# State products in runs of three units, reads in the spare output bank: a schedule change in a fused cross-attention and ReGLU kernel

## The chip, the cores and the metric

The kernel runs on one core of a Trainium2 chip. The metric is device microseconds of one execution, taken as the median of several runs; smaller is better. The profile comes from one further execution, recorded by the hardware profiler.

## What is computed

For each of 8 batches and 8 heads there are 512 tokens `x` (64 wide) and 32 state vectors `state`. Tokens read from the states and states read from the tokens; the two results are joined along the rows, heads are folded into the width (8 x 64 = 512), and a feed-forward block with a rectified gate follows.

```python
# x: (8, 8, 512, 64)   state: (8, 8, 32, 64)
scores = scale * x @ state.T                # tokens to states
a = softmax(scores);   xread = a @ state
scores2 = scale * state @ x.T               # states to tokens
a2 = softmax(scores2); sread = a2 @ x
h = concat([xread, sread], axis=2)          # 544 rows per batch and head
rows = h.transpose(0, 2, 1, 3).reshape(8 * 544, 512)
out = (relu(rows @ w_gate) * (rows @ w_val)) @ w_out     # d_ff = 1536
```

The output is 4352 x 512 in float32. Matmul operands on the chip are bf16.

## The kernel before, in words

The 512 token rows of a batch are not multiplied with the gate and value weights directly. Since `xread = a @ state`, the kernel forms the **state products** U = state times weight once per batch (32 states of 8 heads against 1536 columns, for both weights), and then `a` times U. U is stored in bf16 as (weight w, half kc of the heads, column).

The engines work so. TensorE (PE) does all matmuls and transposes. ScalarE (ACT) does the exponentials, relu and copies out of PSUM. VectorE (DVE) does sums, the gate-times-value product and copies. GpSimd (POOL) converts the inputs and issues some loads; SyncE (SP) issues the others, the transposing DMAs and the stores.

The work is a list of **steps**. A step is one block of 128 columns of d_ff, `jf` 0 to 11, of one batch `b`; its number is g = 12*b + jf. In each step PE runs:

- `gv` (L317, matmuls at L314): four matmuls 128x128x512, two for the gate and two for the value, into two PSUM banks. `relu` (L338, ACT) reads the first bank, `mult` (L342, DVE) the second and the relu's result.
- an **output piece**, `out_piece(b, i)` (matmuls at L351): four of the twelve matmuls that make one output tile of 128 rows. A tile is three pieces, i, i+1, i+2 with i a multiple of 3. Its first piece calls `o_bank` for a PSUM bank, and its last is followed by `fin_x`: a copy on ACT (L359) and a store on SP (L360). The piece issued in step g is number g - 18 (`lag`), again counted in twelves per batch.
- then the **units** that are hung on this step by `at(b, jf, f, ...)`, in the order in which they were added.

The units, with their lines:

- `att_half(b, i)`: scores of one half of the heads (L198, PE), exponential (L205, ACT), sum, reciprocal and scaling (L211, L213, L217, DVE); after the second half the result is transposed by a DMA on SP (L225) into ANS, the stationary partner of U in `gv`.
- `u_block(b, lo)`: state products of 512 columns. It calls `u_unit` (eight matmuls of a 64x32 tile of the array, L289, into two banks) for each weight, and `u_out` (L299) to cast each bank into U: both banks of the gate on ACT, both of the value on DVE. So a run is two units, and a batch has three runs.
- `sr(b)`: the states' read of batch b: 32 matmuls of a 128x32 tile (L262, PE), then `sr_norm` on DVE: a reciprocal (L269) and a multiplication into `sn` (L271).
- `sr_T(b)`: one transpose of `sn` (L275, PE) and a copy on ACT (L276).
- `x_dma`, `x_next`, `x_pad`: load of the tokens of a later batch (SP), conversion on POOL and a transposing DMA on SP, and a padded copy on POOL for the read.
- `state_prep`: transposes of the states of batches 4 to 7 on PE (L127) and copies on ACT (L131).

**Banks.** PSUM has eight banks. `bank(name, kind)` (L81) hands them out: kind "r" goes round banks 0 to 5, kind "o" alternates banks 6 and 7 for output tiles. A bank handed out again is waited for until its last reader is through. The counter of each kind is in `turn`.

Steps up to 27 are an order written out by hand, with the banks of each word. The loop of the change begins at step 28, (2,4), and ends with step 107; steps 96 to 107 are those of the states' rows (`gvs`). Orders within an engine's queue are those of the program.

Of the kernel before, what the change touches and what calls it, by code (L numbers as in the profile page):

```python
# [16 lines left out]
def kernel(  # L17
# [9 lines left out]
    nc = tc.nc  # L27
# [7 lines left out]
    NF = d_ff // 128  # L35
# [19 lines left out]
    NK = 2  # L55
# [7 lines left out]
    NX, DP = 2, 66  # L63
# [15 lines left out]
    given, turn = [], {"r": 0, "o": 0}  # L79

    def bank(name, kind="r"):  # L81

        if given:
            n = given.pop(0)
        else:
            n = turn["r"] % 6 if kind == "r" else 6 + turn["o"] % 2
            turn[kind] += 1
        return psum.tile([128, 512], FP32, name=name, tag=f"b{n}")

    held = {}  # L90
# [33 lines left out]
    def state_T(g):  # L124
        ps = held["st", g] = bank("stT_ps").bitcast(BF16)[:, 0:512]
        for i in range(4):
            nc.tensor.transpose(ps.rearrange("p (q i m) -> p q i m", i=4, m=8)[:, :, i],  # L127
                                st_b[:, g % 3, i].rearrange("p h d -> p (h d)"), id128)
# [31 lines left out]
    def x_T(b, j):  # L160

        if b not in xT:
            xT_alloc(b)
        ps = bank("xT_ps").bitcast(BF16)[:, 0:512].rearrange("p (c t) -> p c t", c=NC)
        for c in range(NC):
            if b == 0 and j < 2:
                nc.tensor.transpose(ps[:, c], x_head(b)[:, c, 2 * j:2 * j + 2].rearrange("p h d -> p (h d)"), id128)
            else:
                v, h = (x_tail(b), 2 * j - HK) if b == 0 else (xb[b], 2 * j)
                for h2 in range(2):  # L170
                    nc.tensor.transpose(ps[64 * h2:64 * h2 + 64, c], v[:, c, h + h2], id128)  # L171
        held["xT", b, j] = ps
# [4 lines left out]
    def x_T2(b, half):  # L177
        if b not in xT:
            xT_alloc(b)
        ps = held["xT2", b, half] = bank("xT_ps").bitcast(BF16).rearrange("p (c j t) -> p c j t", c=NC, j=2)  # L180
        for j in range(2):
            for c in range(NC):
                for h2 in range(2):
                    nc.tensor.transpose(ps[64 * h2:64 * h2 + 64, c, j], xb[b][:, c, 4 * half + 2 * j + h2], id128)  # L184
# [68 lines left out]
            src = src.rearrange("p c h d -> p h c d")  # L253
            nc.gpsimd.tensor_copy(out=v[:, hs:hs + src.shape[1]], in_=src)  # L254

    def sr_mm(b):

        ps = held["sr", b] = bank("sr_ps")[:, 0:2 * DP].rearrange("p (r d) -> p r d", r=2)
        for c in range(NC):
            for parity in range(2):  # L260
                for j in range(NJ):
                    nc.tensor.matmul(ps[32 * j:32 * j + 32, parity, 0:D + 1], e_sn[b][:, parity, c, 32 * j:32 * j + 32],  # L262
                                     xa[:, b % NX, H * c + 2 * j + parity, 0:D + 1],
                                     start=(c == 0 and parity == 0), stop=(c == NC - 1), skip_group_check=True)

    def sr_norm(b):
        ps = held["sr", b]
        rr = small.tile([128, 2], FP32, name="rr", tag="rr")
        nc.vector.reciprocal(out=rr, in_=ps[:, :, D])  # L269
        sn = held["sn", b] = small.tile([128, 2, D], BF16, name="sn", tag="sn")  # L270
        nc.vector.tensor_tensor(out=sn, in0=ps[:, :, 0:D], in1=rr.to_broadcast([128, 2, D]), op=ALU.mult)  # L271
# [20 lines left out]
    def u_unit(b, w, lo):  # L292

        u_alloc(b)
        ps = held["u", b, w, lo] = [bank("up"), bank("up")]
        u_mm(ps, b, w, lo, 512)

    def u_out(b, w, lo, kc, eng):
        copy[eng](out=U[b][:, w, kc, lo:lo + 512], in_=held["u", b, w, lo][kc])  # L299
# [17 lines left out]
    def gv(b, jf):  # L317
        if b not in hsb:
            hsb[b] = hpool.tile([128, NF, S], BF16, name="h_sb", tag="h_sb")
        held["gv", b, jf] = [bank("gv_ps"), bank("gv_ps")], hsb[b][:, jf], S  # L320
        for w in range(2):
            for kc in range(NK):
                gv_mm(held["gv", b, jf][0], b, jf, w, kc)

    def gvs(jf):
        f0 = jf * 128
        ps = [bank("gv_ps"), bank("gv_ps")]
        nt = B * Ns
        for w, wsb in ((0, wg_sb), (1, wv_sb)):
            for j in range(NJ):  # L330
                nc.tensor.matmul(ps[w][:, 0:nt], wsb[:, j, f0:f0 + 128], br[:, j].rearrange("p b n -> p (b n)"),  # L331
                                 start=(j == 0), stop=(j == NJ - 1))
        held["gv", B, jf] = ps, hs_sb[:, jf], nt

    def relu(b, jf):
        ps, dst, n = held["gv", b, jf]
        g_sb = held["g", b, jf] = gpool.tile([128, 512], BF16, name="g_sb", tag="g_sb")
        nc.scalar.activation(out=g_sb[:, 0:n], in_=ps[0][:, 0:n], func=AF.Relu)  # L338

    def mult(b, jf):  # L340
        ps, dst, n = held["gv", b, jf]
        nc.vector.tensor_tensor(out=dst, in0=ps[1][:, 0:n], in1=held["g", b, jf][:, 0:n], op=ALU.mult)  # L342
# [4 lines left out]
    def out_mms(src, b, tsub, jfs):  # L347
        if jfs[0] == 0:
            held["o", b, tsub] = o_bank()
        for jf in jfs:  # L350
            nc.tensor.matmul(held["o", b, tsub], src[:, jf, tsub * 128:(tsub + 1) * 128], wo_sb[:, jf],  # L351
                             start=(jf == 0), stop=(jf == NF - 1))
# [4 lines left out]
    def fin_x(b, tsub, eng="act"):  # L357
        o_sb = opool.tile([128, d_model], FP32, name="o_sb", tag="o_sb")
        copy[eng](out=o_sb, in_=held["o", b, tsub])  # L359
        nc.sync.dma_start(out=out_rows(b, tsub), in_=o_sb)  # L360

    def fin_s(t2):
        outr = out.rearrange("(b s) m -> b s m", s=SP)
        o_sb = opool.tile([128, d_model], FP32, name="o_sb", tag="o_sb")
        nc.scalar.copy(out=o_sb, in_=held["o", B, t2])
        for bq in range(4):
            eng = nc.sync if bq % 2 == 0 else nc.scalar
            eng.dma_start(out=outr[t2 * 4 + bq, S:SP], in_=o_sb[bq * Ns:(bq + 1) * Ns])
# [14 lines left out]
    def out_part(b, i):  # L383
        tsub, q = divmod(i, 3)
        out_mms(hsb[b], b, tsub, list(range(4 * q, 4 * q + 4)))

    def out_piece(b, i):
        out_part(b, i)
        if i % 3 == 2:
            fin_x(b, i // 3)  # L390
# [37 lines left out]
    def spin(n, cols=512):  # L428
        for i in range(n):
# [6 lines left out]
             "sc": att_sc, "ex": att_exp, "nr": att_sum, "nx": att_scale, "aT2": att_T2, "ao2": att_out2, "aT": att_T, "ao": att_out,  # L436
             "c": c_unit, "co": c_out, "u": u_unit, "uo": u_out, "gv": gv, "re": relu, "mu": mult, "o": out_part,
             "of": fin_x, "xn": x_next, "xp": x_pad, "sr": sr_mm, "sn": sr_norm}
    program = """
    dx.1.0.2 dx.1.1.2 stc.0.0.act stc.0.1.dve spin.7 stT.0@0 xc.0.0.dve dw.0.0.128 sto.0.act dw.1.0.128 on xc.0.1.dve  # L440
# [31 lines left out]
        assert not given  # L472


    units = {}

    def at(b, jf, f, *args):
        units.setdefault(NF * b + jf, []).append(lambda: f(*args))

    def u_block(b, lo, engs=("act", "act", "dve", "dve")):  # L480
        for w in range(2):
            u_unit(b, w, lo)
            for kc in range(NK):
                u_out(b, w, lo, kc, engs[2 * w + kc])

    def att_half(b, kc):
        att_up(b, kc)
# [7 lines left out]
        att_scale(b, kc)  # L495

    def sr(b):
        sr_mm(b)
        sr_norm(b)

    def state_prep(lo, hi):
# [2 lines left out]
            state_out(g, "act")  # L504

    first, lag = 2 * NF + 4, 18
    at(2, 4, x_dma, 4, (nc.sync,))
    at(2, 10, state_prep, 4, B)
    for b in range(3, B):
        s, late = b - 1, 2 if b == 3 else 0  # L510
        for i, jf in enumerate((3, 5)):
            at(s, jf + late, att_half, b, i)
        for i, jf in enumerate((7, 9, 11)):
            at(s, jf, u_block, b, 512 * i)
        if b + 1 < B:
            at(s, 9, x_next, b + 1)
            at(s, 9, x_pad, b + 1)
        if b + 2 < B:
            at(s, 10, x_dma, b + 2, (nc.sync,))
    for b in range(B):  # L520
        s, jf = {0: (2, 2), 1: (2, 3), 2: (2, 8), 3: (2, 11)}.get(b, (b - 1, 9))
        if b > 1:
            at(s, jf, sr, b)
        at(*divmod(NF * s + jf + 2, NF), sr_T, b, "act")
    for g in range(first, NF * (B + 1)):
        b, jf = divmod(g, NF)
        gv(b, jf) if b < B else gvs(jf)
        relu(b, jf)
        mult(b, jf)
        if g >= lag:  # L530
            out_piece(*divmod(g - lag, NF))
        for f in units.get(g, ()):
            f()
    for t2 in range(2):
        out_mms(hs_sb, B, t2, list(range(NF)))
        fin_s(t2)
# [33 lines left out]
```

The softmax here doesn't subtract the row's maximum and nothing guards it: scores larger than these inputs give would overflow.

## Time and profile before

| | |
|---|---|
| median of 7 runs | 226.88 us (226.65 to 227.56) |
| the profiled execution | 226.73 us, of which its span 224.9 us |
| PE busy | 219.6 us of the span |
| ACT, DVE, POOL busy | 124.7, 128.3, 53.3 us |
| gv matmuls L314, 384 | 96.6 us busy, 380 ns each |
| piece matmuls L351, 372 | 94.5 us busy, 379 ns each |
| state products L289 in the loop, 64x512, 288 | 14.2 us busy |
| casts of U, L299, DVE and ACT | 36 of 684 ns and 36 of 592 ns |
| longest PE wait | 1.2 us, at the start |

In a timeline line the columns are start and duration in us, engine, line and operation, output and inputs by the program's names, count, and in brackets the idle time ahead of it and what ended it. Matmuls are pipelined, and the profile models their ends, so one matmul's duration of 380 ns overlaps the next; the distance between starts is what a matmul costs. Loads of weights (PEld) run beside matmuls. A busy time is a total over the whole span; an idle time matters only on the engine that sets the end.

### The profile page before, as it was taken

The page shows a single profiled execution, that of the slowest core. Times are in us where ns is not written, and L with a number is a line of the kernel's source. Part 1 is how long each engine was busy: PE and PEld are TensorE (multiplying, and loading weights), DVE is VectorE, ACT ScalarE, POOL GpSimd, SP SyncE. Part 2 cuts the span into 40 slices and gives each one's busy share as a digit, 9 for nine tenths or more (in the row PEclk, how much of TensorE's full clock was granted, in tenths as well). Part 3 has the DMA queues.
Part 4 walks back from the last instruction along what each step waited for, and adds up shares of the span by engine and source line. Part 5 has one row for each costly group of instructions (what it writes and reads, how often), then busy time and mean ns, then how long its engine had stood idle before and what let it go on. Part 6 is the DMA issues. An engine that isn't in the chain of part 4 may idle for free.

```text
span 224.9 us, 4871 instructions
## 1 busy us (share of the span) xinstructions
PE 219.6 (98%) x1967; PEld 105.0 (47%) x1967; DVE 128.3 (57%) x226; ACT 124.7 (55%) x236; POOL 53.3 (24%) x58
## 2 busy tenths in 40 slices
PE   7899999999999999999999999999999999999994
PEld 3444454444544444444444443444444445666543
DVE  3587888667387657754866467656865443222100
ACT  4599877773566655664466455655556444322221
POOL 8798747503343240006000600000000000000000
PEclk9999999999999999999999999999999999999999
DMA  6999999070719612681159213611311111111132
GB/s 149 176 195 196 209 231 278 26 187 3 231 52 199 225 47 69 144 255 51 48 115 252 88 59 66 125 50 47 93 50 47 48 47 50 48 56 75 60 93 93
DMA packets 37799, 25.48 MB, mean 113 GB/s; under 512 B 18864, under 2 KB 33200, under 8 KB 37776
## 3 DMA queue, kind: packets, MB, share of 16 engines
q1 hardware_dynamic: 24912, 16.85, 26.5%
q0 software_dynamic: 11968, 7.47, 21.5%
q10 hardware_dynamic: 896, 0.85, 1.4%
q8 instruction: 15, 0.25, 0.5%
q14 instruction: 8, 0.07, 0.1%
HBM read 18.35 MB, written 8.91 MB: 121 GB/s over the span
## 4 chain that ended last, share of the span: by engine, by line
PE 94%; DMA 3%; ACT 1%; issue 0%; POOL 0%; DVE 0%; POOLq 0%; DVEq 0%
PE o_ps L351 38%; PE gv_ps L314 38%; PE gv_ps L331 5%; PE up L289 4%; DMA xb<-in_x_dram 3%; PE upc L289 2%; PE sc_ps L198 1%; PE sr_ps L262 1%; PE o_ps L377 1%; PE xT_ps L184 1%; PE warm_ps L430 1%; PE aT_ps L233 1%; ACT xT L187 0%; PE srT_ps L275 0%; PE stT_ps L127 0%; PE xT_ps L171 0%
## 5 line engine op out<-in xcount | busy, mean ns | idle before, releaser
L314 PE MATMUL gv_ps<-ans,U 128*128 128x512 bf16 x384 | 96.6, 380 | 0.0
L351 PE MATMUL o_ps<-wo_sb,h_sb 128*128 128x512 bf16 x372 | 94.5, 379 | 0.0
L342 DVE TENSOR_TENSOR h_sb<-gv_ps,g_sb 128x512 bf16<-128x512 f32 x96 | 65.3, 688 | 42.0 <-ACT g_sb L338 40.8
L338 ACT ACTIVATE g_sb<-gv_ps 128x512 bf16<-128x512 f32 (+1 forms) x108 | 63.1, 584 | 47.0 <-PE gv_ps L314 32.3
L351 PEld LDWEIGHTS <-h_sb 128*128 128x128 bf16 x372 | 36.1, 98 | 40.9 <-issue 0.7
L314 PEld LDWEIGHTS <-U 128*128 128x128 bf16 x384 | 34.9, 98 | 41.2 <-issue 4.2
L359 ACT COPY o_sb<-o_ps 128x512 f32<-128x512 f32 x29 | 17.0, 586 | 20.7 <-PE o_ps L351 20.7
L299 DVE CAST U<-up 128x512 bf16<-128x512 f32 x36 | 23.2, 684 | 5.3 <-PE up L289 5.2
L299 ACT CAST U<-up 128x512 bf16<-128x512 f32 x36 | 19.4, 592 | 10.1 <-PE up L289 10.1
L140 POOL CAST xb<-xf 128x1024 bf16<-128x1024 f32 x10 | 10.6, 1084 | 53.4 <-DMA xf<-in_x_dram 52.1
L254 POOL COPY xa<-xb 128x2048 bf16<-128x2048 bf16 (+1 forms) x9 | 15.3, 1710 | 13.4 <-PE sr_ps L262 6.6
L211 DVE TENSOR_REDUCE cs<-e_sn 128x16 f32<-128x512 bf16 x16 | 10.9, 684 | 8.6 <-ACT e_sn L205 8.6
L342 DVE TENSOR_TENSOR hs_sb<-gv_ps,g_sb 128x256 bf16<-128x256 f32 x12 | 5.1, 424 | 15.3 <-PE gv_ps L331 10.5
L205 ACT ACTIVATE e_sn<-sc_ps 128x512 bf16<-128x512 f32 x16 | 9.6, 599 | 5.6 <-PE sc_ps L198 5.5
L309 ACT CAST U<-upc 128x512 bf16<-128x512 f32 (+1 forms) x20 | 9.5, 533 | 1.4 <-PE upc L289 1.3
L289 PEld LDWEIGHTS <-stT 64*32 64x32 bf16 x512 | 4.9, 89 | 11.2 <-issue 10.8
L430 PE MATMUL warm_ps<-hs_sb 128*128 128x512 bf16 x23 | 7.8, 456 | 1.2 <-DVE hs_sb L394 1.2
L217 DVE TENSOR_TENSOR a_sn<-e_sn,rc 128x512 bf16<-128x512 bf16 x12 | 8.3, 692 | 0.6
L198 PEld LDWEIGHTS <-xT 128*128 128x128 bf16 x128 | 5.7, 98 | 3.8 <-ACT xT L175 0.7
L331 PE MATMUL gv_ps<-br,wv_sb 128*128 128x256 bf16 x48 | 7.2, 273 | 0.0
L331 PE MATMUL gv_ps<-br,wg_sb 128*128 128x256 bf16 x48 | 7.2, 273 | 0.0
L289 PE MATMUL up<-wg_sb,stT 64*32 64x512 bf16 x144 | 7.2, 386 | 0.0
(64 smaller groups left out, 129.2 us busy)
## 6 DMA issues: line engine op xcount, KB each, us to landing
out_dram<-o_sb SPq DMA_DIRECT2D x31, 256.0 KB, 2.3
xf<-in_x_dram SPq DMA_DIRECT2D x4, 1024.0 KB, 6.2
wo_sb<-in_moe_w_out_dram POOLq DMA_DIRECT2D x2, 768.0 KB, 15.2
wg_sb<-in_moe_w_gate_dram POOLq DMA_DIRECT2D x5, 256.0 KB, 8.6
wv_sb<-in_moe_w_val_dram POOLq DMA_DIRECT2D x5, 256.0 KB, 10.4
xf<-in_x_dram POOLq DMA_DIRECT2D x1, 1024.0 KB, 15.9
xb<-in_x_dram POOLq DMA_DIRECT2D x3, 256.0 KB, 6.8
xb<-in_x_dram POOLq DMA_DIRECT2D x1, 512.0 KB, 12.3
```

The lines of the kernel that those rows point to most:

```text
L140: copy[eng](out=xb[b][:, :, hs].rearrange("p c h d -> p h c d"), in_=xf[b][:, hs])
L211: nc.vector.reduce_sum(out=cs, in_=e_v, axis=AX.X)
L254: nc.gpsimd.tensor_copy(out=v[:, hs:hs + src.shape[1]], in_=src)
L289: nc.tensor.matmul(dst[parity][32 * j:32 * j + 32], stT[r:r + 64, b, j, 32 * parity:32 * parity + 32], wsb[r:r + 64, j, lo:lo + n], start= ...
L299: copy[eng](out=U[b][:, w, kc, lo:lo + 512], in_=held["u", b, w, lo][kc])
L314: nc.tensor.matmul(ps[w], U[b][:, w, kc, f0:f0 + 128], ANS[b][:, kc].rearrange("p c t -> p (c t)"), start=(kc == 0), stop=(kc == NK - 1))
L331: nc.tensor.matmul(ps[w][:, 0:nt], wsb[:, j, f0:f0 + 128], br[:, j].rearrange("p b n -> p (b n)"), start=(j == 0), stop=(j == NJ - 1))
L338: nc.scalar.activation(out=g_sb[:, 0:n], in_=ps[0][:, 0:n], func=AF.Relu)
L342: nc.vector.tensor_tensor(out=dst, in0=ps[1][:, 0:n], in1=held["g", b, jf][:, 0:n], op=ALU.mult)
L351: nc.tensor.matmul(held["o", b, tsub], src[:, jf, tsub * 128:(tsub + 1) * 128], wo_sb[:, jf], start=(jf == 0), stop=(jf == NF - 1))
L359: copy[eng](out=o_sb, in_=held["o", b, tsub])
L430: nc.tensor.matmul(warm_ps[:, 0:cols], warm[:, 0:128], warm[:, 0:cols], start=True, stop=True)
```

## The change

The state products of batches 3 to 7 are made in two runs of three units in place of three runs of two. `u_block(b, part)` takes three of the six (weight, column) pairs; of each unit the first bank is cast on ACT and the second on DVE. Runs stand at steps (b-1, 7) and (b-1, 10), for batch 3 at (2, 8) and (2, 11). After the units of such a step the next output piece is issued too, and the following step has none; so the run lies between two pieces.

The states' reads of batches 2 to 7 write the bank that the next output tile will get (`kind == "spare"` does not advance the turn), not one of the six. They stand behind the run in the same step: batches 4 to 7 move from step 9 to 10, batches 2 and 3 stay at (2, 8) and (2, 11). `sr_T` follows one step later for batches 4 to 7 (still step 11), two steps later for 2 and 3 as before. Those of batches 0 and 1 stay at (2, 4) and (2, 5).

Batch 3's softmax halves move from steps (2, 5) and (2, 7) to (2, 4) and (2, 6). The load of batch 4's tokens moves from (2, 4) to (2, 6).

```diff
@@ bank @@
         if given:
             n = given.pop(0)
+        elif kind == "spare":
+            n = 6 + turn["o"] % 2
         else:
             n = turn["r"] % 6 if kind == "r" else 6 + turn["o"] % 2
             turn[kind] += 1
@@ sr_mm @@
-    def sr_mm(b):
+    def sr_mm(b, kind="r"):
-        ps = held["sr", b] = bank("sr_ps")[:, 0:2 * DP].rearrange("p (r d) -> p r d", r=2)
+        ps = held["sr", b] = bank("sr_ps", kind)[:, 0:2 * DP].rearrange("p (r d) -> p r d", r=2)
@@ the loop and its units @@
-    units = {}
+    units, paired = {}, set()
-    def u_block(b, lo, engs=("act", "act", "dve", "dve")):
-        for w in range(2):
+    def u_block(b, part):
+        for w, lo in ((0, 0), (1, 0), (0, 512), (1, 512), (0, 1024), (1, 1024))[3 * part:3 * part + 3]:
             u_unit(b, w, lo)
-            for kc in range(NK):
-                u_out(b, w, lo, kc, engs[2 * w + kc])
+            u_out(b, w, lo, 0, "act")
+            u_out(b, w, lo, 1, "dve")
     def sr(b):
-        sr_mm(b)
+        sr_mm(b, "spare")
         sr_norm(b)
-    at(2, 4, x_dma, 4, (nc.sync,))
+    at(2, 6, x_dma, 4, (nc.sync,))
     for b in range(3, B):
-        s, late = b - 1, 2 if b == 3 else 0
+        s, late = b - 1, 1 if b == 3 else 0
         for i, jf in enumerate((3, 5)):
             at(s, jf + late, att_half, b, i)
-        for i, jf in enumerate((7, 9, 11)):
-            at(s, jf, u_block, b, 512 * i)
+        for part, jf in enumerate((8, 11) if b == 3 else (7, 10)):
+            at(s, jf, u_block, b, part)
+            paired.add(NF * s + jf)
     for b in range(B):
-        s, jf = {0: (2, 2), 1: (2, 3), 2: (2, 8), 3: (2, 11)}.get(b, (b - 1, 9))
+        s, jf = {0: (2, 3), 1: (2, 4), 2: (2, 8), 3: (2, 11)}.get(b, (b - 1, 10))
         if b > 1:
             at(s, jf, sr, b)
-        at(*divmod(NF * s + jf + 2, NF), sr_T, b, "act")
+        at(s, jf + (2 if b in (2, 3) else 1), sr_T, b, "act")
+    piece = first - lag
     for g in range(first, NF * (B + 1)):
-        if g >= lag:
-            out_piece(*divmod(g - lag, NF))
+        if piece <= g - lag:
+            out_piece(*divmod(piece, NF))
+            piece += 1
         for f in units.get(g, ()):
             f()
+        if g in paired:
+            out_piece(*divmod(piece, NF))
+            piece += 1
```

## The prediction

> **What bounds the kernel now.** I read the page first: engine totals, then the chain that ended last.
>
> ```profile
> span 224.9 us, 4871 instructions
> PE 219.6 (98%) x1967; PEld 105.0 (47%) x1967; DVE 128.3 (57%) x226; ACT 124.7 (55%) x236; POOL 53.3 (24%) x58
> PE 94%; DMA 3%; ACT 1%; issue 0%; POOL 0%; DVE 0%; POOLq 0%; DVEq 0%
> ```
>
> The end is set by TensorE (PE): 98% busy, 94% of the chain. The view of PE's waits has only 1.2 us and 0.7 us, both ahead of the main loop. So in the loop any PE time saved shortens the run, and any new PE wait lengthens it. Next the PE timeline of two state-product steps (start, duration):
>
> ```profile
> 111.66 1.03 PE L351 MATMUL o_ps<-wo_sb,h_sb 128*128 128x512 bf16 x4
> 112.62 0.41 PE L289 MATMUL up<-wg_sb,stT 64*32 64x512 bf16 x8
> 112.84 0.40 PE L289 MATMUL up<-wv_sb,stT 64*32 64x512 bf16 x8
> 113.17 1.04 PE L314 MATMUL gv_ps<-ans,U 128*128 128x512 bf16 x4
> 114.05 1.03 PE L351 MATMUL o_ps<-wo_sb,h_sb 128*128 128x512 bf16 x4
> 114.91 1.03 PE L314 MATMUL gv_ps<-ans,U 128*128 128x512 bf16 x4
> 115.77 1.03 PE L351 MATMUL o_ps<-wo_sb,h_sb 128*128 128x512 bf16 x4
> 116.73 0.41 PE L289 MATMUL up<-wg_sb,stT 64*32 64x512 bf16 x8
> 116.96 0.40 PE L289 MATMUL up<-wv_sb,stT 64*32 64x512 bf16 x8
> 117.28 0.43 PE L262 MATMUL sr_ps<-xa,e_sn 128*32 128x65 bf16 x32
> 117.65 1.04 PE L314 MATMUL gv_ps<-ans,U 128*128 128x512 bf16 x4
> 118.52 1.03 PE L351 MATMUL o_ps<-wo_sb,h_sb 128*128 128x512 bf16 x4
> ...
> 120.25 1.03 PE L351 MATMUL o_ps<-wo_sb,h_sb 128*128 128x512 bf16 x4
> 121.76 0.23 PE L275 MATMUL srT_ps<-id,sn 128*128 128x128 bf16 x1
> 121.83 1.20 PE L314 MATMUL gv_ps<-ans,U 128*128 128x512 bf16 x4
> 122.87 1.02 PE L351 MATMUL o_ps<-wo_sb,h_sb 128*128 128x512 bf16 x4
> ```
>
> Read starts: a gv group or a piece takes 0.864, a plain step 1.73. Piece to piece with a two-unit run is 2.39: 0.66 over a plain step. The units start 0.225 apart, so two are 0.45 and **entering and leaving the run costs 0.21**. With the read (sr) behind, 118.52-115.77 = 2.75: 1.02. With the transpose srT behind, 122.87-120.25 = 2.62: 0.89.
>
> DVE's timeline of the run with the read, and of step (2,11):
>
> ```profile
> 116.23 0.69 DVE L342 TENSOR_TENSOR h_sb<-gv_ps,g_sb 128x512 bf16<-128x512 f32 x1 [0.84 <-ACT g_sb L338]
> 117.42 1.29 DVE L299 CAST U<-up 128x512 bf16<-128x512 f32 x2 [0.50 <-PE up L289]
> 118.63 0.16 DVE L269 RECIPROCAL rr<-sr_ps 128x2 f32<-128x2 f32 x1
> 118.82 0.29 DVE L271 TENSOR_TENSOR sn<-sr_ps,rr 128x128 bf16<-128x128 f32 x1
> ```
> ```profile
> 73.47 0.69 DVE L342 TENSOR_TENSOR h_sb<-gv_ps,g_sb 128x512 bf16<-128x512 f32 x1 [1.82 <-ACT g_sb L338]
> 74.18 1.29 DVE L299 CAST U<-up 128x512 bf16<-128x512 f32 x2
> ```
>
> A unit is ready for its cast 0.46 after its start (116.96 to 117.42). Casts follow each other every 0.605 ((118.63-117.42)/2), then the reciprocal (0.19 to the next start) and sn (0.29): the read's bank is let go only at 119.11, 1.83 after sr's matmuls start. Before, nothing needs it soon.
>
> **What the Trainium skill says.** "TensorEngine Tiling (Array Packing)", section Key Properties: a change of tiling mode drains TensorE. The 0.21 per run agrees. "TensorE: Matmul & The Clock Gate", Architectural detail: vector and scalar queues are strict FIFO; Part 2, LDWEIGHTS: matmuls stay in program order, only weight loads are pulled ahead. The DVE rows above keep program order; so a waiting piece holds all matmuls behind it. Same page, Part 1: the clock falls only after an idle window of some 3.4 us. The waits I find are shorter, so I charge no slower clock; the trace of before, at full clock, doesn't test that.
>
> **The change part by part.** T is the start of a step's gv.
>
> *Runs and moved transposes, batches 4 to 7.* Before, per batch: 0.66 (step 7) + 1.02 (9) + 0.89 (11) = 2.57. After: a three-unit run 0.66+0.225 = 0.89; one with the read 1.02+0.225 = 1.25; srT alone, 0.06 (58.44 to 58.50 at its first lone place). Sum 2.19. Gain 0.38 x 4 = **1.53**. Moving a piece behind a run changes no count.
>
> *Batch 3.* Before: two plain runs 1.32, the lone read of batch 2 (65.72 to 67.92: 0.47), run with read 1.02: 2.82. After: two runs with reads, 2.50. Gain **0.32**. Its softmax costs the same PE time in steps 4 and 6.
>
> *The spare output bank.* `bank(..., "spare")` takes bank 6 + turn["o"] % 2 without advancing the turn: the bank that the next new output tile will get. A tile is three pieces; its first calls for a bank. Step g issues piece g-18, counted in twelves per batch. For batches 4 to 7 the run lies at (s,10): the pieces are 4 and, behind the run, 5, both inside a tile. The next new tile, piece 6, starts after gv(11), srT and gv(0), 2.6 us later: no wait. But **batch 3's runs are one step later**. At (2,8), g = 32: piece 14 = (1,2) closes a tile; the piece behind the run is (1,3), which opens one, in the very bank that sr has just filled. At (2,11), g = 35: (1,5), then (1,6): the same. The piece must wait for sn on DVE, and behind it on PE stand all later matmuls.
>
> Price at (2,8): units start at T+1.82, 2.05, 2.27 (111.66-0.86 is T of the first run); sr is through and the next matmul could start at T+2.97 (117.65-114.91 = 2.74 with two units, and 0.225). DVE casts one bank of each unit: first at T+1.82+0.46 = 2.28, then two more, so rr at T+2.28+3x0.605 = 4.10, sn ends 4.58. A dependent weight load follows a DVE end by 0.05 (DVE memset end 1.12, load 1.17). Piece at T+4.63: **1.66**. At (2,11) the mult of that step ends late, 74.16 with T = 71.67, i.e. T+2.49, since ACT copies state transposes ahead of its relu. The third unit takes that mult's bank, and DVE's casts start at about T+2.51: sn ends 4.80, piece 4.85: **1.88**. Together 3.54. If overlap is better than read I allow 0.3 less; if a weight load is exposed after each wait, 0.3 more.
>
> *Third units elsewhere.* Six rotating banks: units one and two take four old ones, the third those of this step's gv. At step 7 the mult ends at T+2.25 (111.77+1.28, less 110.80), behind the softmax on DVE; with 0.05 it holds the third unit's second matmul, due at 2.27, by about 0.04: 0.16 for four. Bounds 0 (issue slack) and 0.15 each. At step 10 it ends at T+1.95: nothing.
>
> *srT one step after the read.* It is due at T+4.69; sn ends T+4.58, its weight load can start at 4.63, though lone srT loads 0.21 ahead. The same instruction with no early load (behind a run) costs 0.17 more (0.89-0.66-0.06). I take **0.10** each, 0.40 for four; bounds 0 and 0.25. Behind it wait gv(0) and all else.
>
> *Moved at no cost.* x load of batch 4, from (2,4) to (2,6), on SP: issued after the output store of 61.03, landing 6.2 later, 67.6 against 63; POOL's casts (2.5) end at 70, the transposing DMA (SP, 4.4 to landing) at 75; its scores are due at 81.4. Batch 3's ANS transpose now stands behind that load; even at 67.6+4.9 = 72.5 it precedes gv(3,0) at 74.4. Stores behind these have four buffers. Without that cover each would cost PE its lateness. xT of batch 3 landed by 49, long before step (2,4). Batch 3's DVE softmax (0.69+0.25+0.69) moves one step earlier; the mults behind it have two steps before their banks return. The copy of each tile still leaves in its own step or one earlier. Casts per batch stay six on ACT and six on DVE, kept from the end by 55 and 57% load.
>
> *Sum.* -1.53 - 0.32 + 3.54 + 0.16 + 0.40 = **+2.25**. The profiled execution took 226.73 (span 224.9 plus 1.83 around it), 0.15 under the median of 226.88: 228.98 on its own time, **229.1** against the median.
>
> **Rivals.** *A, forecast:* two waits on the spare bank outweigh fewer mode changes: 228.2 to 230.4 with every bound at its end, likeliest 229.1. For it: PE has no slack, and the DVE rows give the lag. *B, faster:* the spare bank is let go in time, at both places, so the saving shows. It decides where sn's lag behind sr's end falls under about 0.65 us at each of the two places (3.54 less 2.25, halved); the rows show 1.66. Without the waits: 226.88+2.25-3.54 = 225.6. Against it: the casts stand ahead in DVE's program order. *C, about even:* one of the two places doesn't open a tile there: 229.1-1.77 = 227.3; a lag about 0.7 at both would give the time of before. *D, slower still:* third units wait at all ten runs by 0.15 and srT costs 0.25: +1.5-0.16 + 0.6: 231.0; the step-10 mult ending 0.3 early speaks against.
>
> **How the numbers follow.** A 0.77, B 0.07, C 0.07, D 0.09. What a measurement can tell from no change is 0.2%, 0.45 us. Faster 0.07 (B); same 0.03 and slower 0.04 from C; slower in all 0.90. Range 228.1 to 230.4: A with its bounds (228.2 is 229.1 less 0.3, 0.16 and 0.40; 230.4 is 229.1 with 0.3, 0.44 and 0.60), and the nearer edge of D; B, C and most of D stay outside, about 2 in 10 in all with A's tails.
>
> **What would show it.** PE waits for DVE sn (L271) by 1.6 to 1.9 us ahead of o_ps, twice, in steps (2,8) and (2,11), and at no other run; run-to-run costs of 0.89 and 1.25; srT near 0.06 to 0.3. Two PE gaps missing, or the load of batch 4 delaying a gv, would make it wrong.

## The result, and the profile after

The changed kernel takes 228.38 us (median of 15 runs, 227.71 to 229.17) against 226.82 us for the kernel before (36 runs). The ratio is **1.0067, 95% interval 1.0054 to 1.0080**: slower by about 1.5 us. The prediction was slower, 229.1 us, with a range of 228.1 to 230.4.

The page of the changed kernel first (its lines are numbered two higher than before: the piece is L353, the gv L316, the state product L291, sn L273):

```profile
span 226.5 us, 4870 instructions
PE 218.4 (96%) x1967; PEld 106.2 (47%) x1967; DVE 128.5 (57%) x226; ACT 124.7 (55%) x236; POOL 52.8 (23%) x58
PE 90%; DMA 3%; DVE 2%; ACT 1%; POOL 1%; issue 1%; POOLq 0%; DVEq 0%
```

PE is busy 1.2 us less than before (219.6), and yet the span is 1.6 us longer (224.9). The chain now has 2% of DVE and 4 points less of PE. What PE waited for stands in the view of waits:

```profile
PE o_ps L353 <- DVE sn L273: 3.1, 2, 1.6
```

The columns are total, times, longest, in us. The view's other two lines, 1.2 and 0.4 us, lie ahead of the loop, as the two lines of before did. This one is new: two waits of output pieces for sn. The PE timeline shows where, at steps (2,8) and (2,11):

```profile
63.95 1.03 PE L316 MATMUL gv_ps<-ans,U 128*128 128x512 bf16 x4
...
65.77 0.41 PE L291 MATMUL up<-wg_sb,stT 64*32 64x512 bf16 x8
65.99 0.40 PE L291 MATMUL up<-wv_sb,stT 64*32 64x512 bf16 x8
66.21 0.40 PE L291 MATMUL up<-wg_sb,stT 64*32 64x512 bf16 x8
66.54 0.43 PE L264 MATMUL sr_ps<-xa,e_sn 128*32 128x65 bf16 x32
68.62 1.04 PE L353 MATMUL o_ps<-wo_sb,h_sb 128*128 128x512 bf16 x4 [1.65 <-DVE sn L273]
...
72.59 1.03 PE L316 MATMUL gv_ps<-ans,U 128*128 128x512 bf16 x4
...
74.85 0.69 PE L291 MATMUL up<-wv_sb,stT 64*32 64x512 bf16 x8
75.47 0.44 PE L264 MATMUL sr_ps<-xa,e_sn 128*32 128x65 bf16 x32
77.33 1.04 PE L353 MATMUL o_ps<-wo_sb,h_sb 128*128 128x512 bf16 x4 [1.42 <-DVE sn L273]
```

DVE's timeline of the same stretch shows what sn itself stood behind:

```profile
66.28 1.89 DVE L301 CAST U<-up 128x512 bf16<-128x512 f32 x3 [0.33 <-PE up L291]
68.08 0.16 DVE L271 RECIPROCAL rr<-sr_ps 128x2 f32<-128x2 f32 x1
68.27 0.29 DVE L273 TENSOR_TENSOR sn<-sr_ps,rr 128x128 bf16<-128x128 f32 x1
...
74.39 0.69 DVE L344 TENSOR_TENSOR h_sb<-gv_ps,g_sb 128x512 bf16<-128x512 f32 x1 [2.07 <-ACT g_sb L340]
74.99 1.88 DVE L301 CAST U<-up 128x512 bf16<-128x512 f32 x3
76.79 0.16 DVE L271 RECIPROCAL rr<-sr_ps 128x2 f32<-128x2 f32 x1
76.98 0.29 DVE L273 TENSOR_TENSOR sn<-sr_ps,rr 128x128 bf16<-128x128 f32 x1
```

Three casts, the reciprocal, sn: sn ends at 68.56, and the piece starts 0.06 later. Counted from the gv's start (T), the piece that was due at T+2.97 starts at 68.62-63.95 = T+4.67 and at 77.33-72.59 = T+4.74. **The two waits cost 1.70 and 1.77, 3.47 us together.** The page's waits (1.65 and 1.42) are smaller, since they count idle time only: in the first the leaving of the run falls into the wait, in the second 0.29 lies earlier, in a third unit that takes 0.62 (75.47-74.85) to the next start where the others take 0.33.

Batch 4's runs, from the PE timeline, show the other side:

```profile
114.23 1.03 PE L353 MATMUL o_ps<-wo_sb,h_sb 128*128 128x512 bf16 x4
...
115.63 0.46 PE L291 MATMUL up<-wg_sb,stT 64*32 64x512 bf16 x8
116.01 1.04 PE L353 MATMUL o_ps<-wo_sb,h_sb 128*128 128x512 bf16 x4
116.89 1.89 PE L316 MATMUL gv_ps<-ans,U 128*128 128x512 bf16 x8
...
120.34 1.03 PE L353 MATMUL o_ps<-wo_sb,h_sb 128*128 128x512 bf16 x4
...
121.74 0.40 PE L291 MATMUL up<-wv_sb,stT 64*32 64x512 bf16 x8
122.07 0.43 PE L264 MATMUL sr_ps<-xa,e_sn 128*32 128x65 bf16 x32
122.44 1.04 PE L353 MATMUL o_ps<-wo_sb,h_sb 128*128 128x512 bf16 x4
123.31 1.03 PE L316 MATMUL gv_ps<-ans,U 128*128 128x512 bf16 x4
124.17 0.22 PE L277 MATMUL srT_ps<-id,sn 128*128 128x128 bf16 x1
124.23 1.03 PE L316 MATMUL gv_ps<-ans,U 128*128 128x512 bf16 x4
```

The plain run costs 116.89-114.23-1.73 = 0.93, the run with the read 123.31-120.34-1.73 = 1.24, and srT 0.06. Together 2.23 where the three runs of before cost 2.57. So the aim of the change is met in batches 4 to 7: about 0.34 us each. It is lost again, and more, at the two places of batch 3.

### The profile page after: what moved, and what is told of

Read it like the earlier page. It is cut to its first block, busy times and chain, and to the rows that moved or that the text cites. A ratio compares the mean times of both kernels' runs of the same rounds, so it can differ in the third digit from the quotient of the medians.

```text
span 226.5 us, 4870 instructions
## 1 busy us (share of the span) xinstructions
PE 218.4 (96%) x1967; PEld 106.2 (47%) x1967; DVE 128.5 (57%) x226; ACT 124.7 (55%) x236; POOL 52.8 (23%) x58
## 4 chain that ended last, share of the span: by engine, by line
PE 90%; DMA 3%; DVE 2%; ACT 1%; POOL 1%; issue 1%; POOLq 0%; DVEq 0%
PE o_ps L353 38%; PE gv_ps L316 37%; PE gv_ps L333 5%; PE up L291 4%; DMA xb<-in_x_dram 3%; PE upc L291 2%; DVE U L301 2%; PE sc_ps L200 1%; PE o_ps L379 1%; PE sr_ps L264 1%; PE xT_ps L186 1%; PE aT_ps L235 1%; ACT xT L189 0%; POOL xb L412 0%; POOL xb L420 0%
## 5 line engine op out<-in xcount | busy, mean ns | idle before, releaser
L353 PE MATMUL o_ps<-wo_sb,h_sb 128*128 128x512 bf16 x372 | 94.6, 379 | 3.1 <-DVE sn L273 3.1
L316 PE MATMUL gv_ps<-ans,U 128*128 128x512 bf16 x384 | 94.5, 379 | 0.0
L353 PEld LDWEIGHTS <-h_sb 128*128 128x128 bf16 x372 | 35.2, 98 | 43.1 <-DVE sn L273 3.3
L316 PEld LDWEIGHTS <-U 128*128 128x128 bf16 x384 | 35.8, 98 | 40.4 <-issue 0.6
L301 ACT CAST U<-up 128x512 bf16<-128x512 f32 x36 | 18.9, 595 | 9.3 <-PE up L291 9.3
L301 DVE CAST U<-up 128x512 bf16<-128x512 f32 x36 | 22.7, 682 | 2.1 <-PE up L291 1.8
L142 POOL CAST xb<-xf 128x1024 bf16<-128x1024 f32 x10 | 10.1, 1041 | 57.8 <-DMA xf<-in_x_dram 57.8
L291 PEld LDWEIGHTS <-stT 64*32 64x32 bf16 x512 | 5.9, 89 | 11.5 <-issue 10.2
L291 PE MATMUL up<-wv_sb,stT 64*32 64x512 bf16 x144 | 7.4, 379 | 0.0
L291 PE MATMUL up<-wg_sb,stT 64*32 64x512 bf16 x144 | 7.3, 382 | 0.0
```

What stands on the lines that cost most here:

```text
L142: copy[eng](out=xb[b][:, :, hs].rearrange("p c h d -> p h c d"), in_=xf[b][:, hs])
L291: nc.tensor.matmul(dst[parity][32 * j:32 * j + 32], stT[r:r + 64, b, j, 32 * parity:32 * parity + 32], wsb[r:r + 64, j, lo:lo + n], start= ...
L316: nc.tensor.matmul(ps[w], U[b][:, w, kc, f0:f0 + 128], ANS[b][:, kc].rearrange("p c t -> p (c t)"), start=(kc == 0), stop=(kc == NK - 1))
```

## The experiments

Each was timed in five rounds beside the kernel before, and each ratio is to that kernel: the first four on one chip, where it took 227.23 us, the last three on another, where it took 227.27. (The expectations count in microseconds from the 226.8 of the section on the result; so compare the ratios.) The theory is that of the prediction: a piece that opens an output tile waits until DVE lets the spare bank go. The rivals are that the runs of three themselves, the moved loads, or a fixed delay cost the time. In these traces a group shown as "x3" lacks the record of one of its four matmuls. It is not the first one in the lines shown here, which last 1.03 us or more like a full group; so their starts are right.

**The read ahead of the run.** Only the order inside steps (2,8) and (2,11) changes.

```diff
         for part, jf in enumerate((8, 11) if b == 3 else (7, 10)):
+            if b == 3:
+                at(s, jf, sr, 2 + part)
             at(s, jf, u_block, b, part)
...
-        if b > 1:
+        if b > 3:
             at(s, jf, sr, b)
```

> The changed kernel with the read of batches 2 and 3 put ahead of the three-unit run in its step, not behind it. Theory (the piece behind the run waits until DVE lets the spare bank go): the read ends some 0.4 us into the run, DVE makes rr and sn ahead of the three casts, so sn ends about 2.9 us after the step's gv began and the piece, due at 2.97, waits for nothing. The two waits (1.70 and 1.77 us, 3.47 together) go: 228.4 - 3.4 = about 225.0, ratio to the kernel before near 0.992. Rival (the runs of three, the third units' banks or the moved loads are what costs): the order inside the step changes nothing, about 228.4, ratio near 1.007.

Measured: 225.08 us, ratio **0.9912 (0.9882 to 0.9942)**. Its PE and DVE timelines at (2,8):

```profile
65.00 1.03 PE L353 MATMUL o_ps<-wo_sb,h_sb 128*128 128x512 bf16 x4
65.96 0.43 PE L264 MATMUL sr_ps<-xa,e_sn 128*32 128x65 bf16 x32
66.32 0.41 PE L291 MATMUL up<-wg_sb,stT 64*32 64x512 bf16 x8
...
67.10 1.04 PE L353 MATMUL o_ps<-wo_sb,h_sb 128*128 128x512 bf16 x3
67.97 1.89 PE L316 MATMUL gv_ps<-ans,U 128*128 128x512 bf16 x8
```
```profile
66.46 0.17 DVE L271 RECIPROCAL rr<-sr_ps 128x2 f32<-128x2 f32 x1 [0.32 <-PE sr_ps L264]
66.67 0.29 DVE L273 TENSOR_TENSOR sn<-sr_ps,rr 128x128 bf16<-128x128 f32 x1
66.87 1.87 DVE L301 CAST U<-up 128x512 bf16<-128x512 f32 x3
```

sn is through at 66.96, ahead of the piece at 67.10, and no wait for sn is left. The same instructions in another order: the runs of three and the moved loads, which stay, are not what cost the time.

**The spare bank alone.** The kernel before, with the reads in the spare bank and nothing else of the change.

```diff
+        elif kind == "spare":
+            n = 6 + turn["o"] % 2
...
-        sr_mm(b)
+        sr_mm(b, "spare")
```

> The kernel before, with all reads in the spare output bank and nothing else of the change. Theory: at steps (2,8) and (2,11) the next piece opens a tile in the bank of the read also here, one gv later. In the trace of before that piece started 1.24 us after the read in both steps, while sn ended at 68.93 and 75.87 against pieces due at 67.92 and 75.29: waits of about 1.06 and 0.63, so +1.7 us, 228.5, ratio near 1.0075. From batch 4 on the read is in step 9, where the tile has just been opened: no wait. Rival (the bank costs only together with runs of three, or not at all): 226.8, ratio 1.000.

Measured: 228.77 us, ratio **1.0068 (1.0041 to 1.0095)**. Its PE timeline:

```profile
67.39 1.04 PE L316 MATMUL gv_ps<-ans,U 128*128 128x512 bf16 x4
69.33 1.04 PE L353 MATMUL o_ps<-wo_sb,h_sb 128*128 128x512 bf16 x4 [0.90 <-DVE sn L273]
...
75.83 1.04 PE L316 MATMUL gv_ps<-ans,U 128*128 128x512 bf16 x3
77.35 1.04 PE L353 MATMUL o_ps<-wo_sb,h_sb 128*128 128x512 bf16 x4 [0.48 <-DVE sn L273]
```

Without the wait the pieces would start 0.88 after their gv. They start 1.94 and 1.52 after it: late by 1.06 and 0.64, where 1.06 and 0.63 were expected. The bank costs also without any run of three; one gv between read and piece only shortens the wait.

**All reads in the six rotating banks.**

```diff
-        sr_mm(b, "spare")
+        sr_mm(b)
```

> The changed kernel with all six reads in the six rotating banks, as before the change. Theory: the waits of the two pieces (3.47 us) go, but behind three units the next rotating bank is the first unit's, which ACT's cast holds until about 2.93 us after the step's gv began (3.05 in steps (2,8) and (2,11), where ACT copies an output tile first); the read is due at 2.59 (2.88 in step (2,11)). So four waits of 0.34, one of 0.46 and one of 0.17: 2.0 us. 228.4 - 3.47 + 2.0 = 226.9, ratio near 1.000. Rival (the spare bank is not what costs): not under 228.4.

Measured: 227.63 us, ratio **1.0013 (0.9999 to 1.0028)**. From its PE timeline:

```profile
66.02 0.40 PE L291 MATMUL up<-wg_sb,stT 64*32 64x512 bf16 x8
66.81 0.43 PE L264 MATMUL sr_ps<-xa,e_sn 128*32 128x65 bf16 x32 [0.39 <-ACT U L301]
...
119.31 0.40 PE L291 MATMUL up<-wv_sb,stT 64*32 64x512 bf16 x8
119.98 0.43 PE L264 MATMUL sr_ps<-xa,e_sn 128*32 128x65 bf16 x32 [0.27 <-ACT U L301]
```

A read follows the third unit by 0.33 where it is free. Here it follows by 0.79 (late by 0.46) and 0.67 (late by 0.34), as expected, now waiting for ACT's cast of the first unit. So the spare bank has a purpose behind three units, and four of its six uses are free; the two at batch 3 are not.

**Batch 3's casts all on ACT**, to change only what stands ahead of sn on DVE.

```diff
-            u_out(b, w, lo, 1, "dve")
+            u_out(b, w, lo, 1, "act" if b == 3 else "dve")
```

> The changed kernel with batch 3's casts of U all on ACT, so that DVE has none in the two steps where a piece waits. Theory (the length of the wait is DVE's queue ahead of sn): in step (2,8) the read's result is seen 0.2 us after its end, rr and sn follow at once, sn ends near 3.64 us after the step's gv began, the piece starts at 3.69 in place of 4.67; in step (2,11), with the read 0.29 later, at 3.98 in place of 4.74. About 1.0 + 0.75 = 1.75 us less: 226.6, ratio near 0.999. ACT's six casts in a row end by about 5.4, which delays a relu but no bank that PE needs. Rival (the wait is for the read itself, or a fixed delay of the bank): 228.4.

Measured: 226.91 us, ratio **0.9983 (0.9961 to 1.0006)**. Its PE timeline:

```profile
64.16 1.03 PE L316 MATMUL gv_ps<-ans,U 128*128 128x512 bf16 x3
...
67.80 1.04 PE L353 MATMUL o_ps<-wo_sb,h_sb 128*128 128x512 bf16 x3 [0.62 <-DVE sn L273]
...
71.77 1.03 PE L316 MATMUL gv_ps<-ans,U 128*128 128x512 bf16 x4
...
75.70 1.04 PE L353 MATMUL o_ps<-wo_sb,h_sb 128*128 128x512 bf16 x3 [0.62 <-DVE sn L273]
```

The piece starts at T+3.64 in place of T+4.67 (3.69 was expected), and in step (2,11), whose gv starts at 71.77, at T+3.93 in place of 4.74 (3.98). The wait shrinks by what is taken from DVE's queue, so it is no fixed delay of the bank.

**The two moves alone**, in the kernel before.

```diff
-    at(2, 4, x_dma, 4, (nc.sync,))
+    at(2, 6, x_dma, 4, (nc.sync,))
...
-        s, late = b - 1, 2 if b == 3 else 0
+        s, late = b - 1, 1 if b == 3 else 0
```

> The kernel before with only the two moves: batch 3's softmax halves in steps 4 and 6 of batch 2 in place of 5 and 7, and the load of batch 4's tokens issued in step 6 in place of 4. Theory: both are off the path, the same matmuls are issued and no PE wait appears: 226.8, ratio 1.000 within 0.002. Rival (the later load or the earlier softmax delays a gv, a score or a bank): slower by what PE then waits, 0.5 us or more.

Measured: 227.34 us against 227.27, ratio **1.0002 (0.9988 to 1.0015)**: no difference that can be measured. But the trace shows a wait that the theory did not have, here with the mult on DVE that ends it:

```profile
65.55 0.39 PE L314 MATMUL gv_ps<-ans,U 128*128 128x512 bf16 x1
66.35 0.59 PE L314 MATMUL gv_ps<-ans,U 128*128 128x512 bf16 x2 [0.42 <-DVE h_sb L342]
66.78 1.03 PE L351 MATMUL o_ps<-wo_sb,h_sb 128*128 128x512 bf16 x4
```
```profile
65.61 0.68 DVE L342 TENSOR_TENSOR h_sb<-gv_ps,g_sb 128x512 bf16<-128x512 f32 x1
```

The gv takes 1.23 (65.55 to 66.78) and not 0.88: 0.35 lost. The earlier softmax delays a mult on DVE (65.61 to 66.29), and with a run of state products in step (2,7), between this gv and the last, the banks come round in one step. The stretch from the loop's first gv to the end is longer by about as much in this trace (226.0-57.40 = 168.6 us; 224.9-56.70 = 168.2 before), and the interval, which reaches to 0.34 us, leaves room for it. In the changed kernel the run stands in (2,8), and its trace has no such wait of a gv for a mult. So the expectation of no wait failed; the moves are free in the changed kernel, not in themselves.

**The reads' transpose one step earlier**, in the kernel before, for batches 4 to 7.

```diff
-        at(*divmod(NF * s + jf + 2, NF), sr_T, b, "act")
+        at(*divmod(NF * s + jf + (1 if b > 3 else 2), NF), sr_T, b, "act")
```

> The kernel before with the transpose of the reads of batches 4 to 7 one step earlier, in step 10, away from the run of state products in step 11. Theory: behind a run it costs 0.23 us, alone between two gv or pieces 0.06 (in the changed kernel 0.06 even with its operand just ready), so 4 x 0.17 = 0.7 us less: 226.1, ratio near 0.997. Rival (the 0.17 belongs to the leaving of the run and stays with it): 226.8, ratio 1.000.

Measured: 226.47 us, ratio **0.9978 (0.9962 to 0.9994)**. In its timeline the two steps from the piece at 118.70 to that at 122.87 take 4.17; in the kernel before, from 118.52 to 122.87, 4.35. The 0.18 is saved when the transpose leaves the run, so it doesn't belong to the leaving of the run as such.

What it is can be read from the trace of before. Between the gv ahead of such a run and the gv behind it, the two units take four rotating banks and the transpose takes one; with the two banks of the second gv that is seven, and six rotate. So the second bank of that gv is the first bank of the run, which ACT casts into U. Here are the gv's second and third matmul, the third being the first to write that bank, and the cast:

```profile
122.05 0.38 PE L314 MATMUL gv_ps<-ans,U 128*128 128x512 bf16 x1
122.44 0.38 PE L314 MATMUL gv_ps<-ans,U 128*128 128x512 bf16 x1
```
```profile
121.80 0.59 ACT L299 CAST U<-up 128x512 bf16<-128x512 f32 x1
```

The cast, which stands behind the copy of an output tile, ends at 122.39. The third matmul starts 0.05 later and 0.39 after the second, where matmuls of a gv otherwise start 0.216 apart: 0.17 late. The other three places are alike: casts end at 98.63, 146.15 and 169.91, and third matmuls start at 98.68, 146.20 and 169.96. The view of waits doesn't list this wait, since the second matmul's modelled end, 122.43, covers it. In this experiment the transpose's bank is taken a step earlier, and the gv behind the run gets the banks of the gv ahead of it. So the 0.17 is a wait for a bank; this is read from the traces, and no run moves the bank alone.

**The read ahead, and the first run one step later.** On top of the first experiment:

```diff
-        for part, jf in enumerate((8, 11) if b == 3 else (7, 10)):
+        for part, jf in enumerate((8, 11) if b == 3 else (8, 10)):
```

> The changed kernel with the read ahead of the run for batches 2 and 3 (as in the first experiment) and the first run of batches 4 to 7 in step 8 in place of 7, away from the softmax on DVE. Theory: the third unit's wait for its step's mult (0.05 us each, four times) goes too: 0.2 us under the first experiment, about 224.8, ratio near 0.991. Rival (that spacing isn't a wait, or the two runs two steps apart collide in their banks): the same as the first experiment, or above it.

Measured: 224.87 us, ratio **0.9889 (0.9868 to 0.9911)**: faster than the kernel before and than the changed one. From the piece ahead of the first run of batch 4 to the gv behind the run's second piece it takes 2.60 (112.35 to 114.95), against 2.66 in the changed kernel. The trace shows the third unit's wait gone; the times can't tell this version from the first experiment, whose interval overlaps.

## Why the prediction was right, step by step

*What bounds the kernel.* Right: the waits that PE was given lengthened the span, and nothing made them up later. From the loop's first gv to the end, the kernel with the spare bank alone takes 227.0-57.05 = 169.95 us against 168.2 before: 1.75 more, for waits of 1.70.

*Fewer runs, transposes moved.* 1.53 + 0.32 expected. In batches 4 to 7 the runs measure 0.93 (0.88 with the wait of the third unit taken out) and 1.24, the lone transpose 0.06, as forecast. The experiment with the transpose alone confirms its share, 0.18 a batch. So of the 0.38 a batch, 0.21 comes from entering and leaving one run less, and the rest from moving the transpose, which ends the wait for a bank described there. Batch 3's first run, free of the wait in the first experiment, costs 67.97-65.00-1.73 = 1.24 there, and its second as much (71.93 to 74.90), where 2.50 was forecast for both.

*The spare bank.* Right in place, cause and size: steps (2,8) and (2,11) and no others, 1.70 for 1.66 and 1.77 for 1.88. The second is shorter because DVE's first cast starts 0.60 after the late mult's start, T+2.40, not T+2.51: DVE's own operations overlap, as the casts among themselves do. The bank alone costs, the order of read and run removes the cost, and the length follows DVE's queue; three experiments, each within its interval.

*Third units.* 0.04 each was forecast; the four runs at step 7 show 0.05 (116.01-115.63 = 0.38 in batch 4, where a free one takes 0.33).

*The transpose one step after the read.* **This term was mis-sized: 0.40 charged, nothing measured.** The profile of PE's weight loads has the wait that was foreseen:

```profile
124.15 0.10 PEld L277 LDWEIGHTS <-sn 128*128 128x128 bf16 x1 [0.31 <-DVE sn L273]
```

The load comes 0.02 ahead of its matmul at 124.17, not 0.21. Yet the next gv starts 0.06 later, as behind a transpose loaded early. What the prediction read as the price of a late load, the 0.17 behind a run, was not that: in the trace of before it is the wait of the gv's second bank for ACT's cast, and alone between two gv the transpose has no such wait.

*The moves.* The x load was issued at 61.46, batch 4's transposing DMA at 71.01, a microsecond later than worked out, with its scores not before 84.30. No PE wait there.

*The sum again.* With the gain as forecast and the other terms as measured, -1.85 + 3.47 + 0.20 + 0 = +1.82, where +2.25 was forecast; most of the difference is the 0.40 of the transposes. The two profiles agree: from the loop's first gv to the end there are 224.9-56.70 = 168.2 us before and 226.5-56.45 = 170.05 after, about 1.8 more. The loop of the changed execution began 0.25 earlier, after the same instructions in both kernels; there the waits for the first loads differ from one execution to the next, and in the nine traces the loop begins between 56.26 and 57.40. That is the rest of the way from 1.8 to the 1.6 us between the spans. The ratio's interval, 1.2 to 1.8 us, ends just under 1.82, and the measured time lies near the lower end of the forecast range. I have no run that tells whether the last 0.3 is more than such variation.

Of the Trainium skill's sentences that the prediction leaned on, those on order held here: the vector queue kept its order (three casts ahead of sn, although sn was what PE waited for), and PE's matmuls behind the waiting piece stood still. That the 0.21 per run is the drain of TensorE is tested by no run; it stayed the same with three units (0.88 less 3 x 0.225). The clock stayed full (1.000 in the profiled execution) through idle times of 1.65 us, as "TensorE: Matmul & The Clock Gate", Part 1, would have it with its window of some 3.4 us.

## What to carry to other kernels

A "spare" buffer is spare only until its owner's next turn: for each place where it is lent out, count who takes it next and how soon, since one step of shift turned a free loan into a wait of 1.7 us. When the borrower is read by an engine with a queue, price the loan by the whole queue ahead of the reader, and put the borrower first; here the same instructions in another order changed the result from 0.7% slower to 0.9% faster. Count the rotating banks over everything that stands between two users: one bank for a small transpose made seven out of six and cost 0.17 us each time. Such a wait can be missing from the view of waits; then compare the starts of the matmuls one by one. A cost of nothing, found in one schedule, belongs to that schedule: the moved softmax was free with the run in step (2,8) and cost 0.35 us in the trace with it in step (2,7).

## What the runs showed of the hardware that was not expected

A transpose whose weight load comes only 0.02 us ahead of its matmul (124.15 and 124.17) costs no more, 0.06 us, than one loaded 0.21 us ahead (58.23 and 58.44 in the trace of before). The 0.23 that the same transpose costs right behind a run of 64x32 tiles is no price of that neighbourhood: 0.17 of it is the wait for a bank shown with the experiment that moves the transpose. VectorE's casts of 0.69 us start 0.60 apart in a row, so one overlaps the next; a matmul that waits for VectorE or ScalarE started 0.05 to 0.06 us after their end.
